# Transposing DMAs taken out of their split, side work spread over more tiles, and one set of stores moved in an attention and mixture-of-experts kernel

## The chip, the cores and the metric

The kernel runs on one core of one Trainium2 chip. The core has five engines with a queue of instructions each: TensorE (PE, matrix products and transposes through the array, with its weight loads listed apart as PEld), VectorE (DVE), ScalarE (ACT), GpSimd (POOL) and SyncE (SP, which issues most of the DMAs; ACT issues a few). Each engine takes its instructions in the order in which they were written, and waits at the head of its queue for the results it needs. The metric is the device time of one execution in microseconds (us).

## The reference, cut to what matters

Three layers follow one another on 2304 rows (4 sequences of 576) of width 512.

```python
# attention: q, k, v (4, 8, 576, 64), f the decay
cum = cumsum(log(clip(f)))
x = softmax(scale * q @ k.T + cum[:, None] - cum[None], causal) @ v   # -> (2304, 512)
# four experts, all of them used for all rows
p = probs / probs.sum(-1)
for e in range(4):
    out += p[:, e:e+1] * (relu(x @ w1[e]) @ w2[e])      # 512 -> 1024 -> 512
# soft mixture: 32 slots, 4 for each of 8 experts
logits = out @ phi                                       # (2304, 32)
d = softmax(logits, over the rows);  slot_in = d.T @ out # (32, 512)
slot_out[e] = relu(slot_in[e] @ s1[e]) @ s2[e]           # 8 experts, 32 MB of weights
c = softmax(logits, over the slots); y = c @ slot_out    # c: the mixing weights
```

## The kernel before

**Tiles and pairs.** The rows are 18 tiles of 128. Three tiles make a block of 384 rows (`TPB` is 3, `NBLK` is 6), and two blocks make a pair. Attention and expert 0 run interleaved until about 340 us. Experts 1, 2 and 3 follow, each over the three pairs. All large products are made of float16 halves: a value is a high half plus a low half, and a product is three half products. In a pair, a 2 x 2 product over the two blocks is put together from seven products instead of eight (functions `quad` and its relatives, lines 858 to 1095), for which sums of the two blocks are needed. The products go to PSUM banks called `qA`, `qE` and `qF`; DVE and ACT add, rectify and split them (L882, L886, L889, L898 in the one form, L945 to L975 in the other, L1084 to L1128 in the second layer), and their results are the halves for the output products `pso` (L620, L663, L1147). What lies in on-chip memory is called `arena` in all views.

**What orders the work.** Most instructions are written by a planner: each task (`T`) has an engine, a cost, a priority and a list of tasks that it depends on, and the planner simulates the engines' clocks with these costs to choose the order in which the tasks are written and, for some, the engine. A DMA task such as the stores `keep_s` (L2142, issued by SP at L2143) stands in the order where the planner saw its dependences met. For each pair four pieces of sums are stored in `sd` and for each block its rows in `xd`; `load_x` (L2150 to L2155) brings them back when the next expert comes to the pair.

**Side work of the soft mixture.** In expert 3 the final value of each block of three tiles is turned into its share of the soft mixture in small steps, which are written between the products. `post` (L2319) makes the list for one group `j` of three tiles: two steps of transposes (`pt`, evacuated at L2344 and L2346), the logits (`lg`, L2352) with a running maximum and exponential, the transpose of these (`dt`, L2370), the sum into the slots (`sl`, L2377), and two steps for the mixing weights. `ctr` (L2391) transposes the logits (`ct`), takes the softmax over the slots by three DVE operations (L2396, L2397, L2400) and one of ACT (L2399). `csplit` (L2402) splits the result into float16 halves on DVE (L2405, and L2407 once for each tile), and its last line has ACT issue a DMA (L2409) that transposes the halves into `cT`. `cT` is read only at the very end of the kernel by the product `out` (L2687). `between(j)` (L2420) gives these steps to the planner, which puts one after a product of the last pairs. The steps that are not placed when expert 3's pairs are through come back as `rest`.

**The last six tiles** are written by hand (from L2464). `part(k, ms)` writes the output products of tile k (0 to 2 are block 4, 3 to 5 block 5) for the pages `ms` of the hidden layer; each page takes three products. `step(n)` pops n entries of the list `side`, which begins with two steps `sel` (L2253 to L2257, a transpose on PE and a copy on DVE that a later stage uses) and goes on with `rest`. Block 4's own steps follow between the products of tiles 3 and 4, and block 5 is handled tile by tile (`tr0`, `lg0`, `dt0`, `sl0` and so on; a tile's copy is L2337, its exponential L2360).

**The last stage** runs the eight slot experts on 32 rows. Their weights are streamed through whatever pages of on-chip memory are free: `fill` (L2275 to L2289) issues as many loads on SP as there are free pages, and is called each time pages are freed. The products are `fh` and `fo` (L2612 among them), and the stage ends with `out`.

The lines that the change touches:

Of the kernel before, what the change touches and what calls it, by code (L numbers as in the profile page):

```python
# [294 lines left out]
def moe_attention_kernel(ctx: ExitStack, tc: tile.TileContext, q, k, v, f, probs, w1, w2, phi, s1, s2, out):  # L295
    nc = tc.nc
# [6 lines left out]
    KD, KF = DM // 128, F // 128  # L303
    NTILE = NT // 128
    TPB = 3
# [95 lines left out]
    for p in range(B // 2):  # L401
        a, b = 2 * p, 2 * p + 1
# [1589 lines left out]
    with tc.manual_schedule():  # L1992
# [72 lines left out]
        def step(n):  # L2065
            for _ in range(n):
                if side:
                    x = side.pop(0)
                    if x is None:
                        break  # L2070
                    x()
# [48 lines left out]
        def s_place(p, i):  # L2120
            n = len(p_S[p])
            q, o = (p_S[p][i // 2], i % 2 * 2 * NB) if n == 2 else (p_S[p][i], 0)
            return page(q, 3 if n == 2 else 2)[:, o:o + 2 * NB]
# [15 lines left out]
                           s_t.get(j // 2, []))]  # L2139
                  for j in range(NBLK)}  # L2140

        def keep_s(p):  # L2142
            return [T("DMA", 1.0, 90, lambda i=i: nc.sync.dma_start(out=s_d[p][i], in_=s_place(p, i)), s_t[p]) for i in range(4)]  # L2143
        kept_s = {1: keep_s(1), 2: keep_s(2)}
        HOME = 0
        for k, p in (((1, 1), 1), ((1, 2), 2), ((2, 2), 2), (None, HOME)):
            xR[k] = [xT[2 * p], xT[2 * p + 1], xS[p]]
# [13 lines left out]
        for q, p in (("11", xT_page[4]), ("22", xT_page[5]), ("12", xT_page[3]), ("1", hT_p), ("2", hT_p + 3), ("3", wA + 8),  # L2161
# [8 lines left out]
        hq_free[1, 2] = {"12": kept_x[3], "4": kept_x[2]}  # L2170
        end_s1, end_1, _ = halves_tasks(1, w1_1 + e0_t, w2_1 + pw_t, s_t, tmps, plain_t=(w1_p, e0_t, plain_l1),
                                        t_sums=named(sums_1))
        GATE = (), (), (), (), ((2, 0),), ((2, 0),)
        sc.gate = away(*GATE[0])
        w2_2, last = prep_tasks(2, 1, R, [last[0], s_t[2]], e0_t, 59,
# [143 lines left out]
        def post(tiles, step_no):  # L2319
# [82 lines left out]
            def csplit():  # L2402
                bc = c32.unsqueeze(2).to_broadcast([128, TPB, 2, 32])
                o = c16.rearrange("p t (a b) s -> p t a b s", b=2)
                nc.vector.tensor_scalar(out=o[:, w, :, 0, :], in0=bc[:, w], scalar1=C_MUL, scalar2=None, op0=ALU.mult)  # L2405
                for t in range(t0, t0 + N):
                    nc.vector.scalar_tensor_tensor(out=o[:, t, :, 1, :], in0=bc[:, t], scalar=C_MUL,  # L2407
                                                   in1=o[:, t, :, 0, :], op0=ALU.mult, op1=ALU.subtract)
                nc.scalar.dma_start_transpose(out=cT[:, T0:T0 + N, :], in_=c16[:, w].rearrange("p t a s -> p (t a s)"))  # L2409
            return [lambda: tr(0, 2)] + ([lambda: tr(2, 4)] if N > 1 else []) + (  # L2410
                [logits, dtr, slots] if N == 1 else [lambda: logits()(), None, dtr, None, slots, lambda: sums.pop()()]), [ctr, csplit]


        e = E - 1
# [2 lines left out]
        def between(j):  # L2417
            a, z = post(list(range(j * TPB, (j + 1) * TPB)), j)
            wide.update(a[0:2])
            return a + z + [lambda: fill(0)]  # L2420

        def used_up(p):
            if p == 0:
# [22 lines left out]
        for x in range(2):  # L2446
            dyn.free(xT_page[2 * HOME + x], 3)
        mg = page(dyn.alloc(1))
        side += rest
        fill(0)  # L2450
        cells = {}

# [10 lines left out]
            fill(0)  # L2463
        j = NBLK - 1  # L2464
        po = [post([j * TPB + t], j) for t in range(TPB)]
        for ms in ((0, 1), (2, 4), (5, 6), (3, 7)):
            part(0, ms)
            step(2)
        for ms in ((0, 1), (2, 3)):
            part(1, ms)  # L2470
            step(2)
        part(1, (4, 5))
        step(2)
        part(1, (6, 7))
        while side:
            step(1)
        part(2, range(KF))
        for p in (wA + 8, wA + 11):
            dyn.free(p, 3)
        fill(0)  # L2480
        a, z = post(list(range((j - 1) * TPB, j * TPB)), j - 1)
        a = [x for x in a if x] + z
        for k, ms, n in ((3, (0, 1), 1), (3, (2, 3), 1), (3, (4, 5), 1), (3, (6, 7), 1), (4, (0, 1), 2), (4, (2, 3), 2)):
            part(k, ms)
            for _ in range(n):
# [19 lines left out]
        sl0()  # L2505
        part(5, (2,))
        rest.append(lg1())
        part(5, (3,))
        second_w(1)
        part(5, (4, 5))  # L2510
# [214 lines left out]
```

## Time and profile before

| | |
|---|---|
| time, median of 3 runs | 973.23 us (971.72 to 973.63) |
| the profiled execution | 973.74 us, of which the span of instructions 972.0 us |
| PE busy | 924.1 us, 95% of the span (weight loads 635.4) |
| DVE busy | 702.4 us, 72% |
| ACT busy | 507.6 us, 52% |
| POOL busy | 449.6 us, 46% |
| mean granted clock of PE | 0.992 of full speed |
| DMA | 147 MB, mean 151 GB/s |

PE is busy nearly all the time, so each stretch in which it is not busy is worth a look; the other engines have room on average, but not at every place. The share of busy time says nothing of the order in which the engines wait for each other; that stands in the waits and in the timelines, which the rows below are taken from. The granted clock is the share of full speed (2.4 GHz; the other level is 1.2) at which PE was let run.

### The profile page before, as it was taken

How to read it: one execution, taken by the hardware profiler on the slowest of the kernel's cores; microseconds unless marked ns; L12 is line 12 of the kernel's file. 1: busy time of each engine (PE TensorE's matmuls, PEld its weight loads, DVE VectorE, ACT ScalarE, POOL GpSimd, SP SyncE). 2: the span in 40 equal slices, each digit the busy share in tenths (PEclk: the TensorE clock that was granted, in tenths of full speed). 3: DMA queues.
4: the chain of work that ended last, by engine and by line, in shares of the span. 5: the costliest groups of instructions: out<-in, count | busy, mean ns of one | idle time of the engine just before them, and what ended most of it. 6: DMA issues, size and time to landing. Idle time of an engine off the chain costs nothing.

```text
span 972.0 us, 22479 instructions
## 1 busy us (share of the span) xinstructions
PE 924.1 (95%) x9068; PEld 635.4 (65%) x9068; DVE 702.4 (72%) x1338; ACT 507.6 (52%) x1128; POOL 449.6 (46%) x440
## 2 busy tenths in 40 slices
PE   7988999999999999999999999999999999979994
PEld 3567788787878865456868645786868667544331
DVE  7989987879776489858789786868975584543313
ACT  6878888878677475445063833526351341411123
POOL 3998786785754378434068143726551140000000
PEclk9999999999999999999999999999999999999998
DMA  8789999999999642251202444321512043476495
GB/s 225 186 167 179 183 185 193 190 192 163 206 182 223 109 163 98 77 216 44 88 1 66 152 159 144 131 88 54 205 37 100 1 168 100 176 290 199 155 364 195
DMA packets 266232, 147.13 MB, mean 151 GB/s; under 512 B 231024, under 2 KB 231024, under 8 KB 266128
## 3 DMA queue, kind: packets, MB, share of 16 engines
q1 hardware_dynamic: 264000, 145.13, 58.1%
q8 instruction: 71, 1.16, 0.5%
q10 hardware_dynamic: 2128, 0.57, 0.3%
q14 instruction: 33, 0.27, 0.1%
HBM read 89.83 MB, written 14.16 MB: 107 GB/s over the span
## 4 chain that ended last, share of the span: by engine, by line
PE 73%; DVE 13%; ACT 3%; DMA 3%; issue 3%; POOL 2%; SPq 2%; ACTq 0%; DVEq 0%; POOLq 0%
PE qA L945 9%; PE qA L1084 6%; PE pso L620 6%; PE pso L1147 6%; PE psh L599 6%; PE qE L1084 5%; PE qE L945 4%; PE qF L1084 3%; PE pso L663 3%; PE s L1595 3%; PE qA L875 3%; PE pso L1084 2%; PE pv L1684 2%; PE qF L945 2%; DVE arena L552 2%
## 5 line engine op out<-in xcount | busy, mean ns | idle before, releaser
L1084 PEld LDWEIGHTS <-arena 128*128 128x128 f16 x1512 | 147.8, 98 | 21.4 <-issue 1.8
L945 PEld LDWEIGHTS <-arena 128*128 128x128 f16 x1008 | 98.4, 98 | 68.2 <-issue 5.4
L1464 POOL TENSOR_SCALAR arena<-arena 128x384 f16<-128x384 f32 (+5 forms) x75 | 56.6, 757 | 132.1 <-ACT arena L956 76.0
L975 POOL TENSOR_TENSOR arena<-arena 128x384 f16<-128x384 f32 x80 | 80.6, 1018 | 77.6 <-ACT arena L1462 75.8
L945 PE MATMUL qA<-arena 128*128 128x384 f16 x576 | 104.4, 326 | 1.2 <-ACT arena L956 0.8
L599 PE MATMUL psh<-arena 128*128 128x128 f16 x1728 | 101.9, 219 | 0.0
L620 PE MATMUL pso<-arena 128*128 128x512 f16 x432 | 100.3, 383 | 0.0
L1462 ACT ACTIVATE arena<-arena 128x384 f16<-128x384 f32 (+5 forms) x139 | 80.5, 593 | 33.4 <-DVE arena L967 23.9
L599 PEld LDWEIGHTS <-arena 128*128 128x128 f16 x1728 | 97.3, 98 | 0.4
L1636 ACT ACTIVATE arena<-s,mx,qs 128x320 f32<-128x320 f32 (+4 forms) x144 | 91.6, 641 | 4.8 <-POOL arena L1653 1.8
L1653 POOL TENSOR_TENSOR arena<-arena 128x128 f16<-128x128 f32 (+4 forms) x79 | 70.6, 915 | 14.5 <-ACT arena L1462 12.6
L707 POOL TENSOR_TENSOR arena<-arena 128x768 f32<-128x768 f32 (+2 forms) x23 | 46.5, 2025 | 55.3 <-DVE arena L707 37.8
L1616 DVE TENSOR_REDUCE mx<-s 128x1 f32<-128x576 f32 (+4 forms) x76 | 64.5, 850 | 9.0 <-PE s L1595 8.8
L620 PEld LDWEIGHTS <-arena 128*128 128x128 f16 x432 | 40.5, 99 | 44.3 <-issue 1.8
L1595 PE MATMUL s<-arena 128*128 128x128 f16 (+1 forms) x928 | 65.1, 212 | 4.4 <-ACT arena L1636 3.4
L1084 PE MATMUL qA<-arena 128*128 128x256 f16 x576 | 68.8, 273 | 0.0
L1147 PE MATMUL pso<-arena 128*128 128x512 f16 x288 | 63.3, 379 | 0.0
L1595 PEld LDWEIGHTS <-arena 128*128 128x128 f16 x928 | 57.5, 98 | 7.2 <-issue 5.4
L552 DVE SCALAR_TENSOR_TENSOR arena<-arena,wm 128x512 f16<-128x512 f32 x44 | 55.3, 1270 | 1.9 <-ACT arena L549 1.9
L1653 DVE TENSOR_TENSOR arena<-arena 128x64 f16<-128x64 f32 (+4 forms) x69 | 50.7, 774 | 7.3 <-POOL arena L1464 3.7
L2544 POOL MEMSET arena<- 128x1024 f32 x1 | 1.0, 952 | 116.4 <-PE lg L2352 116.4
L945 PE MATMUL qE<-arena 128*128 128x384 f16 x288 | 53.7, 326 | 1.2 <-DVE arena L967 1.2
(271 smaller groups left out, 1903.7 us busy)
## 6 DMA issues: line engine op xcount, KB each, us to landing
arena<-in_moe_w_dram SPq DMA_DIRECT2D x65, 512.0 KB, 4.7
arena<-in_moe_w_dram SPq DMA_DIRECT2D x63, 256.0 KB, 5.0
arena<-xd SPq DMA_DIRECT2D x10, 768.0 KB, 4.2
arena<-sd SPq DMA_DIRECT2D x16, 384.0 KB, 6.0
arena<-in_moe_w_dram SPq DMA_DIRECT2D x6, 1024.0 KB, 6.8
xd<-arena SPq DMA_DIRECT2D x6, 768.0 KB, 7.5
sd<-arena SPq DMA_DIRECT2D x12, 384.0 KB, 5.5
arena<-in_k_dram SPq DMA_DIRECT2D x16, 256.0 KB, 3.6
```

The source lines that it names most:

```text
L552: return lambda: nc.vector.scalar_tensor_tensor(out=wS[e][o][:, 1, c], in0=b, scalar=am[:, 7:8], in1=wS[e][o][:, 0, c], op0=ALU.mult, op1= ...
L599: nc.tensor.matmul(out=ps[:, m, :], lhsT=wt["w1" + a, 0][:, kk, ms], rhs=xT[j][:, b + kk, ts], start=(n == 0), stop=(n == 3 * KD - 1))
L620: nc.tensor.matmul(out=ops[u], lhsT=a[:, m, ts], rhs=wt["w2" + b, 0][:, m, :], start=(m == 0 and z == 0), stop=(m == KF - 1 and z == 2))
L945: nc.tensor.matmul(out=ps[c], lhsT=wS[e][o][:, w, k, ms], rhs=a[z][:, k], start=(first and i == 0), stop=(i == 5), skip_group_check=True)
L975: h_t[q][m] = y = T(LO, {"DVE": 0.55, "Pool": 1.0}, -30, lambda eng: by[eng].tensor_tensor(out=l_, in0=a, in1=h_, op=ALU.subtract), [y], r ...
L1084: nc.tensor.matmul(out=ps[c, t], lhsT=hq[a][x][:, m, ts], rhs=wq[y][:, m, :], start=(first and m == 0 and n == 0), stop=(m == KF // 2 - 1 ...
L1147: nc.tensor.matmul(out=cell[0], lhsT=a[:, m, ts], rhs=wt["w2" + b, e][:, m, :], start=(len(left) == KF - 1 and z == 0), stop=(not left and ...
L1462: nc.scalar.activation(out=out, in_=x, func=AF.Copy, scale=scale)
L1595: nc.tensor.matmul(out=o, lhsT=qT[u][:, 2 * h + w, :], rhs=kT[kk][:, 2 * h + w, k0:k0 + n_], start=(w == 0), stop=(w == 1 and mask is None))
L1616: nc.vector.tensor_reduce(out=mx[:, 0:nh].rearrange("p (a h) -> p a h", a=sv.shape[1]), in_=sv, axis=AX.X, op=ALU.max, negate=True)
L1636: nc.scalar.activation(out=P[:, x], in_=sv[:, x // hb, x % hb], func=AF.Exp, scale=qs[u][:, 4:5], bias=mxs[n][:, 4 + x:5 + x], accum_out=s ...
L1653: by[eng].tensor_tensor(out=t[:, :, d0:d0 + n_], in0=P[:, :, s0:s0 + n_], in1=t[:, :, s0:s0 + n_], op=ALU.subtract)
```

## The change

Five edits, none of which adds or removes arithmetic. The DMA leaves `csplit` and becomes a step of its own, `cturn`. In `between` it is put behind the step that fills free pages. The list of side steps now has `rest` ahead of the two `sel` steps, and is spread otherwise over the products of tiles 0 to 2: tile 0's products come in two runs of four pages with one step behind each, tiles 1 and 2 in runs of two pages with one step or two. For block 4, `cturn` is called after the second tile of block 5 has had its logits. And the stores of the third pair's sums now depend on a late step of expert 1's products as well.

```diff
--- before.py
+++ after.py
@@ -2139,9 +2139,9 @@
                            s_t.get(j // 2, []))]
                   for j in range(NBLK)}

-        def keep_s(p):
-            return [T("DMA", 1.0, 90, lambda i=i: nc.sync.dma_start(out=s_d[p][i], in_=s_place(p, i)), s_t[p]) for i in range(4)]
-        kept_s = {1: keep_s(1), 2: keep_s(2)}
+        def keep_s(p, deps=[]):
+            return [T("DMA", 1.0, 90, lambda i=i: nc.sync.dma_start(out=s_d[p][i], in_=s_place(p, i)), s_t[p] + deps) for i in range(4)]
+        kept_s = {1: keep_s(1)}
         HOME = 0
         for k, p in (((1, 1), 1), ((1, 2), 2), ((2, 2), 2), (None, HOME)):
             xR[k] = [xT[2 * p], xT[2 * p + 1], xS[p]]
@@ -2170,6 +2170,7 @@
         hq_free[1, 2] = {"12": kept_x[3], "4": kept_x[2]}
         end_s1, end_1, _ = halves_tasks(1, w1_1 + e0_t, w2_1 + pw_t, s_t, tmps, plain_t=(w1_p, e0_t, plain_l1),
                                         t_sums=named(sums_1))
+        kept_s[2] = keep_s(2, [end_s1[-1]])
         GATE = (), (), (), (), ((2, 0),), ((2, 0),)
         sc.gate = away(*GATE[0])
         w2_2, last = prep_tasks(2, 1, R, [last[0], s_t[2]], e0_t, 59,
@@ -2406,9 +2407,11 @@
                 for t in range(t0, t0 + N):
                     nc.vector.scalar_tensor_tensor(out=o[:, t, :, 1, :], in0=bc[:, t], scalar=C_MUL,
                                                    in1=o[:, t, :, 0, :], op0=ALU.mult, op1=ALU.subtract)
+
+            def cturn():
                 nc.scalar.dma_start_transpose(out=cT[:, T0:T0 + N, :], in_=c16[:, w].rearrange("p t a s -> p (t a s)"))
             return [lambda: tr(0, 2)] + ([lambda: tr(2, 4)] if N > 1 else []) + (
-                [logits, dtr, slots] if N == 1 else [lambda: logits()(), None, dtr, None, slots, lambda: sums.pop()()]), [ctr, csplit]
+                [logits, dtr, slots] if N == 1 else [lambda: logits()(), None, dtr, None, slots, lambda: sums.pop()()]), [ctr, csplit, cturn]


         e = E - 1
@@ -2417,7 +2420,7 @@
         def between(j):
             a, z = post(list(range(j * TPB, (j + 1) * TPB)), j)
             wide.update(a[0:2])
-            return a + z + [lambda: fill(0)]
+            return a + z[0:2] + [lambda: fill(0), z[2]]

         def used_up(p):
             if p == 0:
@@ -2446,7 +2449,7 @@
         for x in range(2):
             dyn.free(xT_page[2 * HOME + x], 3)
         mg = page(dyn.alloc(1))
-        side += rest
+        side[:] = rest + side
         fill(0)
         cells = {}

@@ -2463,23 +2466,20 @@
             fill(0)
         j = NBLK - 1
         po = [post([j * TPB + t], j) for t in range(TPB)]
-        for ms in ((0, 1), (2, 4), (5, 6), (3, 7)):
+        for ms in ((0, 1, 2, 4), (5, 6, 3, 7)):
             part(0, ms)
-            step(2)
-        for ms in ((0, 1), (2, 3)):
-            part(1, ms)
-            step(2)
-        part(1, (4, 5))
-        step(2)
-        part(1, (6, 7))
+        step(1)
+        for k in (1, 2):
+            for ms in ((0, 1), (2, 3), (4, 5), (6, 7)):
+                part(k, ms)
+                step(1 + (len(side) > 2 * (TPB - k) + 2))
         while side:
             step(1)
-        part(2, range(KF))
         for p in (wA + 8, wA + 11):
             dyn.free(p, 3)
         fill(0)
         a, z = post(list(range((j - 1) * TPB, j * TPB)), j - 1)
-        a = [x for x in a if x] + z
+        a, cturn = [x for x in a if x] + z[0:2], z[2]
         for k, ms, n in ((3, (0, 1), 1), (3, (2, 3), 1), (3, (4, 5), 1), (3, (6, 7), 1), (4, (0, 1), 2), (4, (2, 3), 2)):
             part(k, ms)
             for _ in range(n):
@@ -2505,6 +2505,7 @@
         sl0()
         part(5, (2,))
         rest.append(lg1())
+        cturn()
         part(5, (3,))
         second_w(1)
         part(5, (4, 5))
```

The first place is ACT's queue at the end of expert 3's last pair. L886 is the rectifying copy of a finished product, `qA` and `qE` are product banks; L2399, in the kernel after L2400, is the exponential of the mixing weights; DMA_TRANSPOSE is the issue of the DMA. Before:

```order
L886 ACTIVATE arena<-qE 128x384
L2399 ACTIVATE arena<-arena 128x96
L886 ACTIVATE arena<-arena 128x384
L2409 DMA_TRANSPOSE arena<-arena 128x3x128
L886 ACTIVATE arena<-qA 128x384
L886 ACTIVATE arena<-qE 128x384
L2346 ACTIVATE arena<-pt 128x384 x2
```

After:

```order
L886 ACTIVATE arena<-qE 128x384
L886 ACTIVATE arena<-arena 128x384
L886 ACTIVATE arena<-qA 128x384
L886 ACTIVATE arena<-qE 128x384
L2400 ACTIVATE arena<-arena 128x96
L2412 DMA_TRANSPOSE arena<-arena 128x3x128
L2347 ACTIVATE arena<-pt 128x384 x2
```

The exponential and the issue of this group moved from among the last four copies of the pair to behind all of them.

The second place is DVE's queue in the same stretch. L882 adds two product banks, L889 makes a low half, L2396 to L2400 (after: L2397 to L2401) are the softmax's steps over the bank `ct`, L2405 and L2407 (L2406 and L2408) the split of the mixing weights, L2256 the copy of a `sel` bank, L2383 the sum into the slots, and L669 the end of an output tile. Before:

```order
L2396 TENSOR_REDUCE arena<-ct 128x3
L2397 TENSOR_TENSOR arena<-ct,arena 128x96
L2400 TENSOR_REDUCE arena<-arena 128x3
L882 TENSOR_TENSOR arena<-qA,arena 128x384
L889 SCALAR_TENSOR_TENSOR arena<-arena 128x384
L2405 TENSOR_SCALAR arena<-arena 128x6x32
L2407 SCALAR_TENSOR_TENSOR arena<-arena 128x2x32 x3
L889 SCALAR_TENSOR_TENSOR arena<-qA,arena 128x384
L882 TENSOR_TENSOR qE<-qE,arena 128x384
L889 SCALAR_TENSOR_TENSOR arena<-qE,arena 128x384
L2256 COPY arena<-sel 128x128 x2
```

After:

```order
L882 TENSOR_TENSOR arena<-qA,arena 128x384
L889 SCALAR_TENSOR_TENSOR arena<-arena 128x384
L2383 SCALAR_TENSOR_TENSOR arena<-arena,sl 96x512
L889 SCALAR_TENSOR_TENSOR arena<-qA,arena 128x384
L882 TENSOR_TENSOR qE<-qE,arena 128x384
L889 SCALAR_TENSOR_TENSOR arena<-qE,arena 128x384
L669 SCALAR_TENSOR_TENSOR arena<-pso,pw,arena 128x512
L2397 TENSOR_REDUCE arena<-ct 128x3
L2398 TENSOR_TENSOR arena<-ct,arena 128x96
L2401 TENSOR_REDUCE arena<-arena 128x3
L2406 TENSOR_SCALAR arena<-arena 128x6x32
L2408 SCALAR_TENSOR_TENSOR arena<-arena 128x2x32 x3
```

The seven operations of the mixing weights moved behind the pair's last half and the first output tile; the sum into the slots came in among the halves, and the `sel` copies went further back.

The third place is ACT's queue at the last blocks. The exponential over 128 x 96 is block 4's; L2337 (after: L2338) copies the transposed rows of one tile of block 5, L2360 and L2363 (L2361 and L2364) are that tile's exponentials. Before:

```order
L2399 ACTIVATE arena<-arena 128x96
L2409 DMA_TRANSPOSE arena<-arena 128x3x128
L2337 ACTIVATE arena<-pt 128x4x128
L2360 ACTIVATE arena<-lg,arena 32x128
L2363 ACTIVATE arena<-arena 32x1
```

After:

```order
L2400 ACTIVATE arena<-arena 128x96
L2338 ACTIVATE arena<-pt 128x4x128
L2361 ACTIVATE arena<-lg,arena 32x128
L2364 ACTIVATE arena<-arena 32x1
L2338 ACTIVATE arena<-pt 128x4x128
L2361 ACTIVATE arena<-lg,arena 32x128
L2364 ACTIVATE arena<-arena 32x1
L2412 DMA_TRANSPOSE arena<-arena 128x3x128
```

The issue moved from ahead of the first tile's copy to behind the second tile's exponentials.

Two more moves. On SP the four stores of the third pair's sums, which stood ahead of two stores of `xd` and eight loads of weights (L498), now stand behind them. With the new times of these loads the planner puts two subtractions L975 of expert 1's first pair on DVE that were on POOL, and one L1464 on POOL that was on ACT. PE's own order is the same as before up to the last pair of expert 3.

## Rows read from the trace of the kernel before

**Rows 1.** Busy time by stretch: window, length, PE, PEld, DVE, ACT, POOL, PEclk, DMA share, GB/s

```profile
840.00:860.00 20.00, 16.79 (x119) 9.28 (x116) 11.03 (x30) 6.87 (x18) 0.00 (x0) 1.00 0.18 61
860.00:868.00 8.00, 6.26 (x35) 3.78 (x38) 2.33 (x7) 1.47 (x3) 0.00 (x0) 0.79 1.06 386
880.00:900.00 20.00, 17.78 (x115) 9.05 (x114) 6.97 (x23) 3.00 (x10) 0.00 (x0) 1.00 0.50 137
936.00:940.00 4.00, 4.00 (x41) 1.19 (x37) 1.65 (x6) 1.18 (x2) 0.00 (x0) 1.00 1.06 402
```

**Rows 2.** Waits of PE: engine, line, what it waited for: total us, times, longest

```profile
PE sel L2255 <- DVE arena L889: 2.7, 1, 2.7
PE lg L2352 <- ACT arena L2337: 2.5, 2, 2.2
PE qA L875 <- DVE arena L882: 2.2, 1, 2.2
...
PE qE L945 <- DVE arena L967: 1.2, 1, 1.2
...
PE qA L875 <- ACT arena L898: 0.9, 1, 0.9
```

**Rows 3.** Chain that ended last, 830 to 900 us: start, us, engine, line

```profile
832.49 1.20 ACTq L2409
...
857.66 1.22 ACTq L2409
862.36 2.56 PE pso L663 x6
865.78 1.29 PE pso L663 x6
...
895.33 1.20 ACTq L2409
```

**Rows 4.** Timeline of ACT: start, us, instruction, [idle before it <- what ended that]

```profile
858.93 0.49 ACT L886 ACTIVATE arena<-qA 128x384 f16<-128x384 f32 x1 [2.75 <-issue]
...
896.63 0.60 ACT L2337 ACTIVATE arena<-pt 128x512 f32<-128x512 f32 x1 [2.40 <-issue]
...
905.01 0.36 ACT L2360 ACTIVATE arena<-lg,arena 32x128 f32<-32x128 f32 x1 [2.63 <-DVE arena L2359]
```

**Rows 5.** Timeline of DVE, 854 to 862 us

```profile
854.01 0.25 DVE L2396 TENSOR_REDUCE arena<-ct 128x3 f32<-128x96 f32 x1
...
855.07 0.55 DVE L882 TENSOR_TENSOR arena<-qA,arena 128x384 f32<-128x384 f32 x1
...
857.13 0.50 DVE L2407 SCALAR_TENSOR_TENSOR arena<-arena 128x64 f16<-128x64 f32 x3
...
861.04 0.56 DVE L889 SCALAR_TENSOR_TENSOR arena<-qE,arena 128x384 f16<-128x384 f32 x1 [0.56 <-ACT arena L886]
```

**Rows 6.** Timeline of PE, 855 to 862 us

```profile
855.67 1.14 PE L875 MATMUL qA<-arena 128*128 128x384 f16 x6 [2.24 <-DVE arena L882]
...
861.74 0.61 PE L2255 MATMUL sel<-ident,arena 128*128 128x128 f32 x2 [2.67 <-DVE arena L889]
```

**Rows 7.** Timeline of ACT in expert 1

```profile
431.74 1.06 ACT L507 ACTIVATE arena<-arena 128x1024 f16<-128x1024 f32 x1 [0.85 <-DMA arena<-in_moe_w_dram]
```

**Rows 8.** Timeline of DVE in expert 1

```profile
447.17 2.48 DVE L975 TENSOR_TENSOR arena<-arena 128x384 f16<-128x384 f32 x2
```

**Rows 9.** Waits of SP at the loads of the last stage

```profile
SPq L2289 <- DMA arena<-arena: 3.8, 2, 1.9
```

**Rows 10.** DMA issues: what, engine, count, KB each, us to landing

```profile
arena<-in_moe_w_dram SPq DMA_DIRECT2D x63, 256.0 KB, 5.0
...
arena<-arena ACTq DMA_TRANSPOSE x5, 5.4
```

**Rows 11.** Timeline of SP, its last loads

```profile
942.23 1.55 SPq L2289 DMA_DIRECT2D arena<-in_moe_w_dram  x3
```

**Rows 12.** Timeline of PE, the last products of the slot experts

```profile
950.64 1.92 PE L2612 MATMUL fo<-arena 128*32 128x512 f32 x16
```

## The prediction, made before the changed kernel was run

> **What bounds the kernel now.** I read the busy time by stage first, then the waits of TensorE (PE), then the chain that ended last, then the timelines of the engines around each hole. PE is the bound: even in the emptiest of the late stages, where the last pair of expert 3 ends, it is busy 16.79 of 20 us [rows 1]. So a change of order can only win what PE loses in holes. The list of PE's waits names them, and nearly all of the large ones belong to lines that run after 800 us: 2.7 us ahead of `sel`, 2.5 ahead of `lg`, 2.2 and 0.9 ahead of `qA` L875; from the middle of the kernel there is one of 1.2 us at L945 [rows 2]. The chain says why: at 832.49, 857.66 and 895.33 us it does not run through PE but through ScalarE's queue (ACT), at the line that issues the transposing DMA of the mixing weights [rows 3]. ACT takes its instructions in order, and this one waits for VectorE's (DVE) split of the same weights. The split's last part ran from 857.13 to 857.63 [rows 5], the DMA was issued at 857.66 and held ACT for 1.22 us [rows 3], and the next activation started at 858.93 after 2.75 us in which no result was missing, only its turn [rows 4]. At 896.63 it is the same with 2.40 us [rows 4].
>
> **The change part by part.** No arithmetic is added or removed. One side step per tile group is added (the issue, taken out of `csplit`), so all steps behind it come one place later.
>
> *First hole, 0.9 us (`qA` L875 behind ACT's L898)* [rows 2]. Now the issue stands two side steps behind its split, with the filling of free pages in between, so ACT no longer waits for DVE there; the 1.2 us of the issue itself stay. In exchange the `ct` step of tile group 1 moves in among the products of the last pair. Ends: 0 to 0.88 us gained; I take 0.7.
>
> *Second hole, 2.24 us (855.67)* [rows 6]. PE waits for the addition L882. DVE was free for it at 854.01, when it took up the three small `ct` steps instead, and began it at 855.07 [rows 5]. With `ct` moved behind the first output products, that 1.06 us goes for certain. In its place PE now has the slots product there, work that it must do anyway and that fills part of what is left, 2.24 - 1.06 = 1.18. I take a rest of 0.6, so 1.6 us gained (ends 1.06 and 2.24).
>
> *Third hole, 2.67 us (861.74)* [rows 6]. After the last product of the pair PE did six output products, came to `sel` at 859.07 and waited, since `sel` takes a bank that is only free when DVE's last split (L889, 861.04 to 861.60) is done [rows 5]. Now PE does 18 products before it needs the last quarter's halves, and 24 before a bank is taken. Six take 1.29 us at full clock [rows 3], so twelve more take it from 859.07 to 861.65: even the slow chain of before is just covered, and without ACT's wait of 2.75 us it is shorter. I take all 2.67 (lower end 2.0).
>
> *The clock.* Within 860 to 868 us the granted clock was 0.79 of full speed [rows 1], so PE ran part of it at 1.2 instead of 2.4 GHz; ahead of it PE had stood still for 2.24 and 2.67 us [rows 6]. 8 x 0.21 = 1.7 us of work lost, and the six products at 862.36 took 2.56 us against 1.29 for the next six [rows 3], which is 1.27 of it. With one hole of 0.6 us left I expect the clock to stay up: 1.6 gained (ends 0 and 1.7).
>
> *Fourth hole, 2.2 us (`lg` behind ACT's L2337, the last group's first tile)* [rows 2]. PE waits for a copy of 0.60 us that started at 896.63. ACT was free 2.40 us earlier [rows 4], at 894.23; without the DMA ahead of it the copy ends at 894.83, 2.40 us before it did, and the hole is 2.2. All of it goes (ends 2.0 and 2.2). The issue now stands behind the second tile's exponentials, where nothing that PE waits for at once is queued behind it on ACT.
>
> *The stores of the third pair's sums* move past the other stores and eight weight loads on SyncE's queue (SP). The load ahead of the square sum at 431.74 no longer shares the DMA engines with four stores, so ACT's wait of 0.85 us there goes [rows 7], and with it perhaps the hole of 1.2 us at L945 [rows 2]. Against this the planner, which sees the load come earlier, gives DVE two more of the subtractions L975, in a stretch where two of them took 2.48 us [rows 8]. Ends: 1.2 gained, 2.5 lost; I take 0.3 gained, since the new DVE order puts one large operation fewer ahead of the sum that frees the hole's bank.
>
> *Side work spread over three tiles* instead of one and a half: the steps hide behind output products that need nothing from them; no cost, as in before. If a copy came late, the cover of one step is six products, 1.29 us [rows 3].
>
> Sum: 0.7 + 1.6 + 2.67 + 1.6 + 2.2 + 0.3 = 9.1 us, less 0.3 for waits of the moved steps that no row shows = 8.8 us. The profiled execution took 973.74 us, 1.7 more than its span of 972.0; it becomes 964.9. The median of the runs is 0.5 us lower, 973.23, so the forecast is 973.23 - 8.8 = 964.4 us.
>
> A rule speaks against two of these terms. The Trainium skill, DMA: Bandwidth & Descriptors, section Issuing engines are not separate DMA queues, says that which engine starts a DMA matters only for the sequencer's time, usually small beside the DMA. By that rule the first and fourth hole would not move, and the sum would be 5.9 us. Here the trace disagrees: what ACT loses at the issue is not its 1.2 us but 2.75 and 2.40 us of standing still ahead of the next activation [rows 4].
>
> **The rivals.**
>
> *The waits come back among the products.* Tile groups 1 and 2 now have steps in the last pair's four quarters that lay elsewhere before (`ct` of 1, and `pt`, `lg`, `dt`, `sl` of 2, each later). There ACT and DVE hand each product on within a microsecond. If five of them each cost what the first hole cost, 0.9 us [rows 2], that is 4.4 us: gain 4.4, 968.8 us. For it: holes one and two lie in these quarters. Against: both had a cause of their own, ACT's wait and `ct` ahead of L882.
>
> *The weights become the bound.* Between 936 and 940 us the DMA engines are full, 402 GB/s [rows 1], feeding the last feed-forward stage. If earlier products only meet weights that are not there, the gain melts to 0 to 2 us: 972 us. Against: the engines were busy only half of 880 to 900 us [rows 1], so 10 us of that stretch alone are spare, more than the gain.
>
> *Slower: the late transposing DMA holds the weight loads.* SP waited twice, 3.8 us in all, for a transposing DMA before it could issue a load [rows 9]. Such a DMA takes 5.4 us to land [rows 10]. The last one went out at 895.33 [rows 3] and now follows the second tile's exponential at 905.01 [rows 4], 10 us later in PE's work, at the start of the final feed. If SP must wait there for both, 15.4 us, the last load comes that much later: it was issued by 943.78 [rows 11] and takes 5.0 us [rows 10], and the last products begin at 950.64 [rows 12], so 1.9 us are spare. 15.4 - 1.9 - 8.8 = 4.7 us slower, 977.9 us. It decides from a hold of about 11 us on. Against: the loads held so far stood close behind a transposing DMA in a burst; this one has few loads around it. The Trainium skill, DMA: Bandwidth & Descriptors, section Rules for kernel authors, advises to issue a DMA early and to wait on it late; by it, moving the issue back is the wrong way round, and no row here shows what that costs.
>
> *It does not do what it says:* the split is late by more than the steps in between, and ACT waits at the new place as at the old. Then only the third hole and half the clock go, 3.5 us: 969.7 us. Against: the split took under 1 us [rows 5], and the steps in between stand for at least six products.
>
> **How the numbers follow.** The forecast has 0.68, waits among the products 0.15, no effect on ACT's wait 0.05, weights as the bound 0.06, held loads 0.06. All upper ends together (0.88 + 2.24 + 2.67 + 1.7 + 2.2 + 1.2 = 10.9) give 962.3; the lower ends (0 + 1.06 + 2.0 + 0 + 2.0 - 2.5 = 2.6) give 970.7. The range of 962.0 to 969.8 us takes in the forecast, the first rival and the last; the weights, the held loads and most of the lowest ends are left out. About 0.2%, 2 us, is what a measurement of this kernel can tell from no change. Faster by more: 0.68 + 0.15 + 0.05 = 0.88; within: 0.06; slower: 0.06.
>
> **What would show it.** In the profile after: no entry of `sel` and of `lg` L2352 over 0.5 us in PE's waits; the chain without ACT's DMA line after 800 us; a granted clock of 1.00 from 840 to 900 us; a hole of at most 1.2 us ahead of the last `qA` product. New entries of L875 waiting for ACT or DVE at other places would be the first rival; SP waiting several microseconds for a transposing DMA, and PE for weights, the slower one. The forecast is wrong if the holes are gone and the last feed-forward stage has become longer, or if expert 1's second pair shows new holes of over 2 us.

## The result and the profile after

| | before | after |
|---|---|---|
| median | 972.79 us (971.0 to 974.4, 6 runs) | 961.44 us (961.02 to 964.72, 6 runs) |
| ratio | | 0.9889, 95% interval 0.9871 to 0.9906 |
| span of the profiled execution | 972.0 us | 959.3 us |
| busy PE, DVE, ACT, POOL | 924.1, 702.4, 507.6, 449.6 us | 921.3, 700.9, 506.7, 447.7 us |

The kernel is 11.35 us faster. The forecast was 8.8 us faster, and 961.44 lies 0.6 us below the low end of the range: the direction was right and the size was wrong.

PE's waits in the profile after, from the same list as [rows 2] (line numbers from 2142 on are shifted by one or two):

```profile
PE qE L1084 <- DVE arena L1095: 0.6, 1, 0.6
PE qA L875 <- DVE arena L882: 0.4, 1, 0.4
...
PE lg L2353 <- ACT arena L2338: 0.3, 1, 0.3
```

The entries of `sel`, of `qA` behind ACT's L898 and of `qE` L945 behind DVE's L967 are gone; `lg` fell from 2.5 to 0.3 us and `qA` behind L882 from 2.2 to 0.4. None of them has come back at another line. The chain that ended last has no issue of a DMA by ACT behind 800 us any more, where it had three [rows 3].

The windows that answer to [rows 1], in the same columns (the last one is 13 us earlier, as its stage is):

```profile
840.00:860.00 20.00, 19.57 (x130) 10.54 (x129) 11.25 (x29) 6.00 (x16) 0.00 (x0) 1.00 0.47 160
860.00:868.00 8.00, 8.00 (x65) 4.10 (x63) 3.05 (x9) 1.53 (x5) 0.00 (x0) 1.00 1.05 383
880.00:900.00 20.00, 19.53 (x101) 8.64 (x98) 7.80 (x26) 3.05 (x10) 0.53 (x1) 1.00 0.52 164
923.00:927.00 4.00, 4.00 (x38) 1.17 (x41) 1.64 (x7) 0.97 (x2) 0.00 (x0) 1.00 1.05 402
```

From 840 to 860 us PE is busy 19.57 us where it was busy 16.79, and from 860 to 868 us the granted clock is 1.00 where it was 0.79. The DMA engines are full in the last stage as before, but no wait came of it.

ACT's queue around the DMA that is now a step of its own, to be held against [rows 4]:

```profile
852.55 0.49 ACT L886 ACTIVATE arena<-qE 128x384 f16<-128x384 f32 x1 [1.13 <-DVE qE L882]
858.32 0.28 ACT L2400 ACTIVATE arena<-arena 128x96 f32<-128x96 f32 x1 [5.29 <-DVE arena L2398]
859.71 1.20 ACTq L2412 DMA_TRANSPOSE arena<-arena  x1
861.01 0.49 ACT L2347 ACTIVATE arena<-pt 128x384 f32<-128x384 f32 x1 [2.41 <-DVE arena L2345]
...
883.73 0.58 ACT L2338 ACTIVATE arena<-pt 128x512 f32<-128x512 f32 x1
...
892.55 1.20 ACTq L2412 DMA_TRANSPOSE arena<-arena  x1
```

The issue of 1.20 us is there at full length, but the last copy of the pair (852.55) is through 6.7 us before it, and the last group's first copy (883.73) has nothing ahead of it.

Where the 12.7 us between the two spans came from is read by taking the start of the same PE instruction in both traces. Before:

```profile
426.19 3.09 PE L945 MATMUL qA<-arena 128*128 128x384 f16 x18
...
447.14 1.14 PE L945 MATMUL qA<-arena 128*128 128x384 f16 x6
...
820.27 1.14 PE L875 MATMUL qA<-arena 128*128 128x384 f16 x6
...
897.28 1.06 PE L2352 MATMUL lg<-arena 128*32 128x128 f32 x8 [2.22 <-ACT arena L2337]
```

After:

```profile
425.44 3.09 PE L945 MATMUL qA<-arena 128*128 128x384 f16 x18
...
444.58 1.14 PE L945 MATMUL qA<-arena 128*128 128x384 f16 x6
...
817.61 1.14 PE L875 MATMUL qA<-arena 128*128 128x384 f16 x6
...
884.59 1.06 PE L2353 MATMUL lg<-arena 128*32 128x128 f32 x8
...
937.99 1.92 PE L2613 MATMUL fo<-arena 128*32 128x512 f32 x16
```

The lead of the kernel after is 0.75 us at the first pair of expert 1 (before anything has changed: in the profiles of all the runs the lead at this point lies between 1.2 us behind and 0.9 us ahead), 2.56 behind it, 2.66 at the start of expert 3's last pair, 12.69 at the last group's first logits, and 12.65 at the last products [rows 12]. So 1.8 us were won in 20 us of expert 1, 10.0 us between 820 and 897 us, and nothing else moved. The second stretch in both kernels, in the columns of [rows 1]:

```profile
820.27:897.28 77.01, 68.95 (x447) 38.18 (x445) 34.66 (x92) 19.14 (x48) 0.00 (x0) 0.98 0.67 231
817.61:884.59 66.98, 66.55 (x448) 37.86 (x445) 34.08 (x91) 18.62 (x48) 0.00 (x0) 1.00 0.75 267
```

The four holes of PE, 8.01 us before, are one of 0.43 us after, and PE needs 2.40 us less of busy time for the same products.

### The profile page after: what moved, and what is told of

It is laid out like the page before. It is cut to its first block, busy times and chain, and to the rows that moved or that the text cites. A ratio compares the mean times of both kernels' runs of the same rounds, so it can differ in the third digit from the quotient of the medians.

```text
span 959.3 us, 22465 instructions
## 1 busy us (share of the span) xinstructions
PE 921.3 (96%) x9068; PEld 635.2 (66%) x9068; DVE 700.9 (73%) x1340; ACT 506.7 (53%) x1127; POOL 447.7 (47%) x439
## 4 chain that ended last, share of the span: by engine, by line
PE 77%; DVE 13%; issue 3%; POOL 2%; ACT 2%; SPq 1%; DMA 1%; DVEq 0%; ACTq 0%; POOLq 0%
PE qA L945 9%; PE psh L599 7%; PE pso L620 7%; PE qA L1084 7%; PE pso L1147 6%; PE qE L1084 5%; PE qE L945 5%; PE pso L663 3%; PE qF L1084 3%; PE qA L875 3%; PE s L1595 3%; PE pv L1684 3%; PE pso L1084 2%; PE qF L945 2%; DVE arena L552 2%
## 5 line engine op out<-in xcount | busy, mean ns | idle before, releaser
L945 PEld LDWEIGHTS <-arena 128*128 128x128 f16 x1008 | 98.4, 98 | 66.5 <-issue 3.8
L1464 POOL TENSOR_SCALAR arena<-arena 128x384 f16<-128x384 f32 (+5 forms) x76 | 56.9, 751 | 135.9 <-ACT arena L956 76.0
L975 POOL TENSOR_TENSOR arena<-arena 128x384 f16<-128x384 f32 x78 | 78.4, 1014 | 75.4 <-ACT arena L1462 73.9
L945 PE MATMUL qA<-arena 128*128 128x384 f16 x576 | 104.5, 326 | 0.7 <-ACT arena L956 0.3
L1653 POOL TENSOR_TENSOR arena<-arena 128x128 f16<-128x128 f32 (+4 forms) x79 | 69.5, 902 | 12.7 <-ACT arena L1462 10.9
L956 ACT ACTIVATE arena<-qA 128x384 f32<-128x384 f32 x48 | 23.3, 486 | 57.7 <-PE qA L945 56.6
L945 PE MATMUL qE<-arena 128*128 128x384 f16 x288 | 53.7, 326 | 0.1
```

The costliest lines, as they stand in the source:

```text
L945: nc.tensor.matmul(out=ps[c], lhsT=wS[e][o][:, w, k, ms], rhs=a[z][:, k], start=(first and i == 0), stop=(i == 5), skip_group_check=True)
L975: h_t[q][m] = y = T(LO, {"DVE": 0.55, "Pool": 1.0}, -30, lambda eng: by[eng].tensor_tensor(out=l_, in0=a, in1=h_, op=ALU.subtract), [y], r ...
L1653: by[eng].tensor_tensor(out=t[:, :, d0:d0 + n_], in0=P[:, :, s0:s0 + n_], in1=t[:, :, s0:s0 + n_], op=ALU.subtract)
```

## The experiments

Each kernel was timed in five rounds beside the kernel before; intervals are 95%.

**The stores alone.**

```diff
-        kept_s = {1: keep_s(1), 2: keep_s(2)}
+        kept_s = {1: keep_s(1)}
...
+        kept_s[2] = keep_s(2, [end_s1[-1]])
```

> The kernel before with the one edit of the stores (third pair's sums stored once expert 1 is through). Theory: the gain before 800 us belongs to this edit alone, and it is two holes, 0.46 us at 434 us and 1.18 us at 446 us, with their restarts 1.7 us in all: ratio about 0.9982, lead of PE over before grows by 1.7 us between 430 and 447 us and by nothing after that. Rival A (the prediction's term): only 0.3 us, ratio 0.9997, and the 1.7 us seen in the profile is drift between executions. Rival B: the late stages gain too, because other pages come free earlier: more than 2.5 us.

Measured 971.89 us against 972.84, ratio 0.9995 (0.9985 to 1.0005). In its trace the two holes of expert 1 are gone and PE gains 1.8 us there, but the execution had lost 1.2 us in attention. The times do not confirm the 1.8 us (the interval's end is 1.5) and do not refute a part of it; three more experiments on the stores follow below.

**The transposing DMA as a step of its own, without the rest.**

```diff
+
+            def cturn():
                 nc.scalar.dma_start_transpose(out=cT[:, T0:T0 + N, :], in_=c16[:, w].rearrange("p t a s -> p (t a s)"))
...
-            return a + z + [lambda: fill(0)]
+            return a + z[0:2] + [lambda: fill(0), z[2]]
```

> The kernel before with the transposing DMA as a step of its own, two steps behind its split, for the groups that the planner places and for those that are left over; block 4's stays directly behind its split, the side list and the stores are as before. Theory: the first hole (0.88 us) goes, and the second (2.24) shrinks to about 0.4, since the third group's softmax steps fall out of the pair; with the restarts 3 us. The third hole (2.67) stays or shrinks a little, the clock's loss stays, the fourth (2.2) stays: ratio 0.995 to 0.997. Rival: the holes 1 and 2 come back inside the pair, since other side steps move up to their places: 0 to 1 us, ratio about 0.9995.

967.56 us, ratio 0.9948 (0.9935 to 0.9961): 5.1 us, more than the 3 expected. In the waits of PE `qA` behind L898 is gone, `qA` behind L882 is 0.4, and `sel` fell from 2.7 to 0.6, which I had expected to stay. The fourth hole stays at 2.2.

```profile
PE sel L2255 <- DVE arena L889: 0.6, 1, 0.6
PE qA L875 <- DVE arena L882: 0.4, 1, 0.4
```

**The side work spread over three tiles, without the rest.**

```diff
-        side += rest
+        side[:] = rest + side
...
+        for ms in ((0, 1, 2, 4), (5, 6, 3, 7)):
+            part(0, ms)
+        step(1)
```

> The kernel before with the side list in the new order and spread over three tiles; the transposing DMAs stay behind their splits and the stores are as before. Theory: the third hole (2.67 us) and its restart go; if the clock falls because of the third hole its 1.7 us go as well, 4.5 us in all, ratio 0.9953; if the second hole (2.24 us), which stays, is enough to bring the clock down, 2.8 us, ratio 0.997. Rival: ACT's wait for the split still delays the last half, so the hole moves to the products behind the 24 that need nothing: under 1.5 us, ratio above 0.9985.

970.44 us, ratio 0.9981 (0.9971 to 0.9990): 1.8 us. The third hole is gone: 30 output products run without a break behind the pair's last product. The second stays at 2.2, and the clock stayed at 1.00 after it.

```profile
856.17 1.14 PE L875 MATMUL qA<-arena 128*128 128x384 f16 x6 [2.23 <-DVE arena L882]
857.14 1.14 PE L875 MATMUL qE<-arena 128*128 128x384 f16 x6
858.11 6.64 PE L663 MATMUL pso<-arena 128*128 128x512 f16 x30
```

By the times the 2.8 us of the case without the clock is the end of the interval, and 4.5 us are refuted. Between the two profiled executions it is 4.6 us, 1.7 of it because the clock fell in the one of before and not in this one. Why the times show less is open; the paragraph on the clock below has a possible reason.

**Block 4's DMA alone.**

```diff
-        a = [x for x in a if x] + z
+        a, cturn = [x for x in a if x] + z[0:2], z[2]
...
         rest.append(lg1())
+        cturn()
```

> The kernel before with block 4's transposing DMA alone moved behind the second tile's logits. Theory: the fourth hole, 2.2 us ahead of the last group's first logits, goes, and nothing else moves: ratio 0.9977, and the last feed-forward stage is shifted as a whole. Rival A (held loads): SP waits for the late DMA and the last stage grows by what the hole gave: ratio 1.000. Rival B (which engine issues a DMA does not matter): the hole stays, ratio 1.000 as well, with the wait of PE still in the list.

969.86 us, ratio 0.9976 (0.9964 to 0.9989): 2.3 us, as expected; the wait of `lg` is 0.3. The late DMA goes out at 900.35 us, and SP waits behind no transposing DMA after that (its one such wait, 2.2 us, is before 885 us). Rivals A and B fall.

**The stores cut at their old place.** Their bytes are an eighth, into a buffer that nobody reads; the real stores come late. The order of the other engines is that of before.

```diff
+        early = [T("DMA", 1.0, 90, lambda i=i: nc.sync.dma_start(out=s_cut[i], in_=s_place(2, i)[:, 0:96]), s_t[2]) for i in range(4)]
```

> The order of PE, DVE, ACT and POOL is that of the kernel before, instruction by instruction; on SP the four stores of the third pair's sums are cut at their old place to an eighth of their bytes (96 of 768 columns, into a buffer that nobody reads), and the real stores are made late, as in the changed kernel. Theory 1 (traffic): the load that ACT waits for at 431.7 us lands earlier, since it no longer shares the DMA engines with the stores, and both holes in expert 1 (0.46 and 1.18 us) go with the order unchanged: lead of 1.6 to 1.8 us there, ratio 0.9983. Theory 2 (order): only the planner's other order of DVE and ACT fills the second hole: ACT's wait of 0.85 us and the hole of 0.46 go, the hole of 1.18 stays; lead of 0.5 us, ratio 0.9995.

972.77 us, ratio 0.9996 (0.9986 to 1.0005). ACT no longer waits for the load, but PE's timeline shows that this gave nothing:

```profile
433.42 2.11 PE L945 MATMUL qA<-arena 128*128 128x384 f16 x12
436.18 1.14 PE L945 MATMUL qA<-arena 128*128 128x384 f16 x6 [0.65 <-DVE arena L962]
...
446.32 0.97 PE L945 MATMUL qE<-arena 128*128 128x384 f16 x5 [1.18 <-DVE arena L967]
```

The hole of 0.46 us went and one of 0.65 came; the hole of 1.18 stands as it was. Taking the traffic away gains nothing as long as the order stays.

**The other order with the stores' traffic.** Four full stores into an unread buffer are made early, all else as with the edit of the stores.

```diff
+                if not s_left:
+                    for i in range(4):
+                        nc.sync.dma_start(out=s_cut[i], in_=s_place(2, i))
```

> The counterpart of the run with the stores cut: the order of PE, DVE, ACT and POOL is that of the kernel with the edit of the stores alone, and four stores as large as the old ones are made at the old place into a buffer that nobody reads (the real ones late). Theory (order): the hole of 1.18 us at 446 us stays away though ACT waits for its load again, so the lead there is 1.0 to 1.8 us as with the edit; ratio 0.998 to 0.9995. Rival (traffic and order both needed): with the load late both holes are back, no lead, ratio 1.000.

972.2 us against 973.4, ratio 0.9985 (0.9973 to 0.9997). The lead grows by 1.4 us in expert 1: it loses 0.4 at a new hole of 0.27 us at 426.24, and wins 1.8 behind it, where both old holes are gone.

```profile
414.02 5.35 SPq L2154 DMA_DIRECT2D scut<-arena  x4
...
426.24 3.09 PE L945 MATMUL qA<-arena 128*128 128x384 f16 x18 [0.27 <-ACT arena L956]
...
430.86 1.06 ACT L507 ACTIVATE arena<-arena 128x1024 f16<-128x1024 f32 x1 [0.38 <-DMA arena<-in_moe_w_dram]
```

The old place was not quite hit: the stores went out at 414.02, against 419.45 us in the kernel before, and the load that ACT waits for came 0.9 us earlier than there. So for the second hole it is shown that the order fills it. For the first, an early load alone did not win anything (the run before this one) and the new order with a load this early did; the new order with the load as late as before was not run. DVE's timeline shows how the order works at the second hole. Before:

```profile
442.69 1.34 DVE L967 SCALAR_TENSOR_TENSOR arena<-arena 128x384 f32<-128x384 f32 x2
444.05 0.56 DVE L967 SCALAR_TENSOR_TENSOR arena<-qA,arena 128x384 f32<-128x384 f32 x1
444.52 0.55 DVE L1037 SCALAR_TENSOR_TENSOR arena<-qE,arena 128x384 f16<-128x384 f32 x1
445.09 0.57 DVE L962 TENSOR_TENSOR qF<-qF,arena 128x384 f32<-128x384 f32 x1
445.57 0.55 DVE L967 SCALAR_TENSOR_TENSOR arena<-qE,arena 128x384 f32<-128x384 f32 x1
```

In the run with the new order and the stores' traffic:

```profile
442.32 0.54 DVE L1037 SCALAR_TENSOR_TENSOR arena<-qE,arena 128x384 f16<-128x384 f32 x1
442.78 0.70 DVE L967 SCALAR_TENSOR_TENSOR arena<-arena 128x384 f32<-128x384 f32 x1
443.40 0.54 DVE L967 SCALAR_TENSOR_TENSOR arena<-qE,arena 128x384 f32<-128x384 f32 x1
```

The operation of L967 that reads `qE`, and so frees the bank for the next product, stood behind five others (counted from the addition L962 that reads `qA`) and ended at 446.12; now it stands behind two and ends at 443.94, before the product comes to it.

**The whole change without the stores, and the whole change again.**

> The changed kernel without the edit of the stores. Theory: the holes in expert 1 are back and the late stages are those of the changed kernel: 1.7 us slower than the whole change in the same job, ratio to before about 0.9906. Rival (what the single run of the edit measured, 0.5 us): ratio 0.9894. Second rival: with the late stages shorter the edit is worth nothing, 0.9889.

> The changed kernel again, beside the kernel before and the one without the edit of the stores, to have its ratio from more executions: 0.989, 961.4 us. If the first six executions were lucky in the attention stage, whose start differs by about 1 us from execution to execution, up to 0.990.

Without the stores 963.41 us (962.87 to 964.15), ratio 0.9898 (0.9885 to 0.9910); the whole beside it 961.60 (961.50 to 962.09), ratio 0.9881 (0.9868 to 0.9894). The times of the two do not overlap (one of the six executions in the table at the top took 964.72, though): the stores' edit is worth 1.8 us here, as the traces say. Expert 1's two holes, 0.5 and 1.2 us, are back in the kernel without it.

**SP issues the DMA instead of ACT.** One word differs from the kernel before.

```diff
-                nc.scalar.dma_start_transpose(out=cT[:, T0:T0 + N, :], in_=c16[:, w].rearrange("p t a s -> p (t a s)"))
+                nc.sync.dma_start_transpose(out=cT[:, T0:T0 + N, :], in_=c16[:, w].rearrange("p t a s -> p (t a s)"))
```

> The kernel before with SP instead of ACT issuing the transposing DMAs of the mixing weights; all else is as before, the split stays directly ahead of the issue, and the order of PE, DVE and POOL is unchanged. Theory (ACT's wait for the split is what costs): the first and fourth hole (0.88 and 2.2 us) go, the third (2.67) falls to about 0.6 as in the run with the DMA as a step of its own, the second (2.24, DVE's softmax steps ahead of the addition) stays: 5 to 5.5 us, ratio 0.9945. Rival (it does not matter which engine issues, the split itself is late): holes stay, ratio 0.999 to 1.000. Rival (SP is held now): the weight loads of the last stage come later than the products want them: ratio above 1.000 with SP waiting for DVE and PE for loads.

967.04 us, ratio 0.9940 (0.9927 to 0.9953): 5.8 us by this word. Its waits of PE:

```profile
PE qA L875 <- DVE arena L882: 2.2, 1, 2.2
...
PE sel L2255 <- DVE arena L889: 0.8, 1, 0.8
...
PE lg L2352 <- ACT arena L2337: 0.3, 1, 0.3
```

Holes one and four are gone and the third is 0.8, while the second, which is DVE's, stands at 2.2. SP waits now at this line (31.4 us at the longest) and the weights still come in time. Both rivals fall.

**An empty step instead of the DMA's own.** The side steps have the places that they have in the run with the DMA as a step of its own; the DMA stays behind its split.

```diff
-            return a + z + [lambda: fill(0)]
+            return a + z + [lambda: fill(0), lambda: None]
```

> The kernel before with an empty step put behind each group's steps: the places of all side steps among the products are those of the run with the DMA as a step of its own, DVE's order is the same as there, but the DMA stays directly behind its split. It tells the displacement of the steps from the separation of the DMA. Theory: the second hole falls from 2.24 to 0.4 us and the third from 2.67 to about 0.6, both by displacement, since the third group's steps leave the pair; the first hole (ACT behind the split, 0.88) stays or comes back at another product: ratio 0.9955 to 0.996, about 1 us less than that run's 5.1. Rival (separation did it): holes 2 and 3 stay, ratio above 0.998.

967.61 us, ratio 0.9935 (0.9922 to 0.9948): as fast as the run with the DMA as a step of its own. PE's timeline:

```profile
837.92 1.14 PE L875 MATMUL qE<-arena 128*128 128x384 f16 x6 [0.20 <-DVE arena L889]
...
853.71 1.14 PE L875 MATMUL qA<-arena 128*128 128x384 f16 x6 [0.43 <-DVE arena L882]
...
857.73 0.41 PE L2255 MATMUL sel<-ident,arena 128*128 128x128 f32 x2 [0.62 <-DVE arena L889]
```

Holes two and three shrink as expected; the first, which I had expected to stay, is down to 0.20, though ACT still stands idle for 2.27 us around the issue there. In the pair it is the displacement of the steps that pays, not the distance between split and issue.

**One edit more.** In the changed kernel the rescaling factor of the running sums is made one step later, its use two steps later.

```diff
-                if step_no:
...
+                if step_no and N == 1:
+                    scale()
+                    total()
...
                 nc.vector.tensor_copy(dT[:, R], p[:, 0:32 * N])
+                if step_no and N > 1:
+                    scale()
...
+                if step_no and N > 1:
+                    total()
```

> The changed kernel with one more edit: for the groups of three tiles the rescaling factor of the running sums (a subtraction on DVE, an exponential on ACT) is made in the step of the transpose and its sum in the step of the slots, no longer in the step of the logits, where DVE stands 0.48 us waiting for ACT with the pair's operations queued behind it. Theory (what is left among the products is again an engine that waits in order): the hole of 0.57 us ahead of the product at 812.6 us goes and that of 0.43 us at 849.8 us goes or shrinks; with the restarts 0.6 to 1.3 us: 960.2 to 961.0 us, ratio 0.987. Rival: the holes only move one step on, ratio 0.988 as the changed kernel.

> The changed kernel once more, beside the version with the further edit, so that these two are told apart in one job: 961.5 us, ratio 0.9881; the version with the further edit below it by 0.6 to 1.3 us, or by nothing.

961.82 us, ratio 0.9880 (0.9867 to 0.9893), and the whole change beside it 961.42 us, 0.9874 (0.9859 to 0.9889): nothing gained. The hole of 0.57 us fell to 0.34 and that of 0.43 grew to 0.62: DVE's operation of 0.20 us that was moved away from ahead of one addition now stands ahead of the next. No version tried beats the changed kernel.

## Why the prediction was wrong, and where it was right

**The step that failed** is the term of the stores: "Ends: 1.2 gained, 2.5 lost; I take 0.3 gained". It measured 1.8 us, above its own upper end: in the traces of the changed kernel and of both its repeats, and in the times of the kernels with and without this edit. The reason that the prediction gave last, DVE's new order with fewer operations ahead of the one that frees the bank, is what the two runs with the stores cut and with the stores' traffic show (three fewer, not one); the reason that it gave first, the shared DMA engines [rows 7], won nothing by itself. This step is 1.5 us of the miss, about half of it. The size failed for three things. The upper end was one hole of [rows 2], though a second one of 0.46 us at 434.08, ahead of L945 behind ACT's L956, hung on the same queues. The subtractions L975 moved to DVE were charged at their most crowded [rows 8], two in 2.48 us, while those of this stretch in the kernel after take 0.55 to 1.04 us each. And I let a gain and a loss nearly cancel that came from one and the same order, instead of counting in it what stands ahead of the operation that frees the bank.

**The holes of the last pair and block** came out as forecast or somewhat fuller: 0.88 for 0.7, 1.81 for 1.6, 2.67 for 2.67, 2.22 for 2.2, and the clock 1.7 for 1.6. That is 9.3 of the 10.0 us between the two landmarks. The other 0.7 us was in no term: of the 2.40 us of PE's busy time that went, the clock is only 1.7. A part of it is that a product behind a hole takes longer than the next one, as the chain of the kernel before shows.

```profile
834.65 1.14 PE qA L875 x6
835.79 0.66 PE pt L2342 x6
836.44 0.97 PE qA L875 x6
```

That is 0.17 us for this start. Where nothing but one hole went, PE won 1.04 us for the first hole of 0.88 (the run with SP) and 2.29 for the fourth of 2.22 (the run with block 4's DMA alone), so these two starts cost 0.16 and 0.07 us; the second hole has kept a start, with its rest of 0.43. What makes up the remainder of the 0.7 us is not shown. I had also set 0.3 us the other way, for waits that no row shows; none came. So by the two traces the sum was short by 1.5 us at the stores, 1.3 at the late holes and 0.3 at the reserve, 3.1 in all. Even its upper ends together, 10.9 us, lie below the 11.9 us that the traces show behind the attention stage. By the medians the gain is 11.35 us, 2.55 more than forecast; the half microsecond between the two is inside the interval. The median of before, with more runs, is 0.44 us lower than the one the forecast started from, which makes the miss 3.0 us.

**Why the holes went** was only partly as told. For the first and third hole two remedies work singly: SP as the issuer, or one more step per group. The prediction gave the third hole to the number of products ahead of `sel`; the run with the work spread shows that this suffices, and the runs with SP and with the empty step that neither spreading nor more products are needed. So the edits overlap, and the gains of the single runs (0.5, 5.1, 1.8 and 2.3 us) cannot be added up to a gain of each. The fourth hole has one cause, the DMA ahead of the copy: both runs that took it out of ACT's way there closed the hole. With SP as the issuer, ACT's activation that came at 858.93 us after 2.75 us of idle time [rows 4] comes after 0.67 us, in which it waits for its product, and the kernel is 5.8 us faster. The Trainium skill, DMA: Bandwidth & Descriptors, section Issuing engines are not separate DMA queues, says that starting DMAs from several engines saves only the sequencer's time for the start, usually small beside the DMA itself. The run with SP disagrees with its 5.8 us.

**The clock.** The term was right for this pair of profiles, but it is not bound to the holes. With the second and third hole as in the kernel before, the run with the stores alone had a granted clock of 1.00 from 840 to 872 us, and for that reason alone its lead grew by 1.7 us there. In the runs with block 4's DMA alone and with the stores cut it fell at 856 us, within a microsecond of the end of the second hole, and the slower products there filled part of the third, which was 1.0 instead of 2.7: that fall cost nothing. In the run with the stores cut it fell a second time, behind the fourth hole, where no large hole followed to take it up:

```profile
895.72 1.06 PE L2355 MATMUL lg<-arena 128*32 128x128 f32 x8 [2.23 <-ACT arena L2340]
896.71 2.70 PE L663 MATMUL pso<-arena 128*128 128x512 f16 x6
...
898.00:900.00 2.00, 2.00 (x7) 0.55 (x6) 0.71 (x2) 0.00 (x0) 0.00 (x0) 0.50 0.00 0
```

The six products at 896.71 took 2.70 us, against 1.47 in the kernel before, and the lead shrank by 1.6 us. So of five profiles with the holes of before, the clock fell around the second and third hole in three, and a fall costs between nothing and 1.7 us, by what stands behind it. This makes single traces poor scales: the run with block 4's DMA alone won 4.0 us between the two profiled executions and 2.3 by the times. It may also be why the spread side work won only 1.8 us: a fall behind its second hole would find no third hole to hide in. No profile shows that case.

**The rivals.** Waits among the products: two of 0.6 and 0.4 us, the first of which was there before, instead of 4.4 us. Weights as the bound: the last stage moved by 12.65 us as a whole. Held loads: at the loads of the last stage SP's waits after have no entry for a transposing DMA, where there were 3.8 us [rows 9]. No effect on ACT's wait: the waits above show it gone.

One sentence of the section on the change has to be set right: tile 0's two runs of products are followed by one step together, as the diff has it, and not by one each.

## What to carry to other kernels

When an order of instructions changes, look in each engine's queue for the one operation that frees the bank or buffer the bound engine waits for, and count what stands ahead of it in both orders: here that gave 1.8 us, where the bytes of the moved stores gave nothing. A DMA issued by a compute engine costs that engine the whole wait for its data, here 2.75 and 2.40 us for an issue of 1.2; give it to a queue with nothing urgent behind it, or put other steps between. And a hole costs its length plus the slower start behind it, up to 0.17 us here, while several edits that close the same hole pay only once.

## What was not expected of the hardware

The granted clock fell to 0.50 at 862 us in one execution and not at all in another with the same two holes of 2.2 and 2.7 us. In two others it fell within a microsecond of the end of the hole of 2.2 us, before any third hole, and in one of these again behind a single hole of 2.23 us. And a queue that waited long cost nothing by itself: SP stood 31.4 us at one transposing DMA, with other loads queued behind it, in a kernel that was 5.8 us faster.
